# The leaky rectifier of a feed-forward layer as one activation with a slope

## The chip, the core and the metric

The kernel runs on one core of a Trainium2 chip. The metric is the device time of one execution in microseconds. TensorE (PE) multiplies matrices, VectorE (DVE), ScalarE (ACT) and GpSimd (POOL) work on tiles of 128 partitions, and SyncE (SP) issues the transfers.

## The reference

Attention keeps the 32 largest scores of each row, then two feed-forward layers follow. The first has a leaky rectifier with slope 0.01, the second a squared rectifier.

```python
# q, k, v: (4, 8, 576, 64); 2304 tokens of 512 features; both layers 512 -> 2048 -> 512
scores = scale * np.matmul(q, k.transpose(0, 1, 3, 2))
kth = np.partition(scores, -top_k, axis=-1)[..., -top_k:-top_k + 1]     # top_k = 32
scores = np.where(scores >= kth, scores, -1000000000.0)
attn = softmax(scores); x = attn @ v                                    # as (2304, 512)
h = x @ w_in;  g = np.maximum(0.01 * h, h);       x = g @ w_out         # first layer
h = x @ w_in2; r = np.maximum(h, 0.0); g = s * (r * r) + b
out = g @ w_out2                                                        # second layer
```

## The kernel before

**Precision.** TensorE multiplies float16. Each operand is held as the sum of two float16 halves: the high half is the rounded value, the low half the rest. A product takes three matmuls (high by high, high by low, low by high). Weights arrive as float64 bits and are turned into halves in the first 200 us; those of the first layer stay on the chip, those of the second go to device memory and are streamed back for each block, except two pairs that stay ("kept").

**Attention.** A unit is a pair of heads for 128 queries; there are 18 tiles of 128 queries and 4 units in each, 72 in all. For a unit and head, TensorE computes 128 x 576 scores (line 768) and ScalarE copies them to s (L774). VectorE finds the 32 largest by four rounds of MAX8 (L786) with three MATCH_REPLACE8 between (L795). ScalarE takes the exponential (L808), and VectorE's mask (L811) keeps what is at least the 32nd largest score and sums it. ScalarE and GpSimd make the halves (L865, L869), a transposing DMA turns them (L873; the first 7 units go through TensorE instead), TensorE multiplies by the values (L897), and VectorE scales the result into x (L904), after a small GpSimd step (L820, L823) and a reciprocal (L826).

**The feed-forward layers.** The 18 tiles form 14 blocks: ten of one tile and four of two (blocks 10 to 13). A layer of a block begins with `rows_in`: ScalarE's square with a sum (L940), a power of two on VectorE (L298, L303), a scaled copy (L944), the high half (L947), GpSimd's low half (L950), and a transposing DMA (L968), for each tile. Then it goes through groups g of 512 columns of h: TensorE computes h (L1022, in packets of 12 matmuls), the rectifier makes it g in halves, and TensorE adds g times the second weights to acc (L1093, packets of 3 matmuls). The second layer's rows come from acc of the first.

**The rectifier of the first layer**, for each of its 72 groups: ScalarE's a1 (L1050) reads h with a positive scale and clips, a2 (L1054) does it with -0.01 times the scale, into a tile of ring r2 that lies in the common tile `early`. GpSimd's a3 subtracts one from the other (L1058). Then a4 (L1067) makes the high half on ScalarE and a5 (L1070) the low half on GpSimd:

```python
nc.scalar.activation(box["r1"], box["h"], AF.Relu, scale=cg[:, 2 * l, 3, gi:gi + 1])
nc.scalar.activation(box["r2"], box["h"], AF.Relu, scale=cg[:, 1, 3, g * nf // 4:g * nf // 4 + 1])
nc.gpsimd.tensor_tensor(box["r1"], box["r1"], box["r2"], op=ALU.subtract)
```

In the second layer a1 clips, GpSimd squares for the low half (L1062), and ScalarE squares for the high one (L1067).

**What sets the order.** A planner, `Plan`, holds each step with its engine, a price in us, what it waits for, the buffers of rings that it takes, and a key. `order()` plays all steps through in time: whenever an engine is free, it takes the ready step with the lowest key. The instructions of each engine are then written in that order, and at run time each engine works through its own list in order. The feed-forward steps of a1 to a5 have the lowest keys of all (-200); matmuls of the layers have keys that grow with the block and the layer, so a change of prices or steps in one place can change the order anywhere behind it. The tables of offsets at the top of the file (`KO`, `W0`, `WD`) are keys, too.

Of the kernel before, what the change touches and what calls it, by code (L numbers as in the profile page):

```python
# [21 lines left out]
# buffers of each ring of tiles  # L22
# [3 lines left out]
# who takes the low halves of the weights: P the tensor engine, D the vector engine, G GpSimd  # L26
WM = {"1i": "PPP", "1o": "P", "2i": "PG", "2o": "DP"}
ORDER = ("1i", "1o", "2i", "2o")
# loads of weights before all others
WF = 0  # L30
EB = 7
# rows of which layers are turned by a transfer
# [3 lines left out]
# offsets of keys: loads of weights, halves of weights, keys, values, queries, the first units  # L36
KO = {"wl": 8.18, "wh": 1.24, "k": -17.94, "v": -14.26, "q": -62.89, "u0": -7.18, "u1": -1.77, "u2": -1.7, "kt": -23.91, "qh": -4.87}
NB = 10
# pairs of blocks of the second layer that stay on the chip
NRES = 2  # L40
DEBUG = []
# from the end of a step to the start of one that waits for it
# [5 lines left out]
# from the issue of a transfer to its start  # L48
# [8 lines left out]
class Plan:  # L57
    """Steps of single engines with what they need, put into a static order: each engine takes, whenever it is free,
    the ready step with the lowest key. A token is a buffer of a ring, taken by its first step and free after its last."""
# [7 lines left out]
    def token(self, ring):  # L67
        self.by_tok.append([ring, 0])
        return len(self.by_tok) - 1
# [19 lines left out]
    def order(self):  # L89
# [17 lines left out]
        while events:  # L107
# [13 lines left out]
            for e, q in ready.items():  # L121
                while q and free[e] <= now + 1e-9:
# [16 lines left out]
                    if e == "SP":  # L139
                        # transfers are issued one by one, wait for each other and take their time  # L140
                        end = moved = max(now + self.issue[n] + LAG, moved) + self.dur[n]
# [25 lines left out]
def kernel(  # L167
# [35 lines left out]
    def open_phase(name):  # L203
        # the pool of the weights' way in makes room for the one of the weights' way round
# [9 lines left out]
    # rings in a common tile: what the beginning needs lies where something else comes later  # L214
# [42 lines left out]
    # ------------------------------------------------ constants  # L257
# [26 lines left out]
    def inv2(dst, src):  # L284
        # dst = 1 / src for powers of two
        nc.vector.tensor_scalar(dst.bitcast(I32), src.bitcast(I32), -1.0, float(254 << 23), op0=ALU.mult, op1=ALU.add)

    def chain(eng, todo, deps, key, take=(), use=()):
        # steps one after the other: (price, function)
# [5 lines left out]
    def pow2_steps(dst, src, step=1, dur=0.07):  # L295
        # dst = a power of 2 (of 4: step 2) with dst * sqrt(src) in [2^-1/2, 2^1/2) ([2^-3/2, 2^1/2))
# [10 lines left out]
    # ------------------------------------------------ the weights: float64 bits to float32, then to scaled halves  # L307
    # a scale for each four blocks
# [15 lines left out]
    for m, f in order:  # L324
# [14 lines left out]
        def w_shift(m=m, f=f):  # L339
            # the low seven exponent bits and the fraction move up by three  # L340
# [4 lines left out]
        def w_rest(m=m, f=f):  # L345
            # the fraction's next bits, rounded, as an integer in the last place
# [862 lines left out]
```

## Time and profile before

| | us |
|---|---|
| median of 3 runs | 1252.0 |
| lowest run | 1249.91 |
| highest run | 1602.58 |
| span of the profiled execution, first to last instruction | 1250.3 |
| busy in it: TensorE, VectorE, ScalarE, GpSimd | 1070.3, 1036.9, 827.4, 842.1 |

No time of the profiled execution other than its span is given; the span lies between two of the runs. The third run, 1602.58, stands far from the other two and is not used. Busy times overlap, since the engines run side by side; a step counts for the end only where other engines wait for it.

### The profile page before, as it was taken

The numbers are of one execution on the slowest core, as the hardware profiler recorded it, in microseconds if no ns is written. First come the engines' busy times: TensorE is split into PE (matmuls) and PEld (weight loads), VectorE is DVE, ScalarE is ACT, GpSimd is POOL, SyncE is SP. The second block draws the span as 40 slices with busy tenths as digits, with TensorE's granted clock in tenths as the row PEclk, the third lists the DMA queues.
The fourth block names the chain that finished last, engine by engine and source line by source line (L and its number), as shares of the span: only waits on it lengthen the run. The fifth ranks groups of instructions, "written<-read, shape, count | busy, mean of one in ns | idle before, by whom it ended". The sixth has DMA issues, their size and how long they took to land.

```text
span 1250.3 us, 27997 instructions
## 1 busy us (share of the span) xinstructions
PE 1070.3 (86%) x10520; PEld 735.6 (59%) x10520; DVE 1036.9 (83%) x2437; ACT 827.4 (66%) x1427; POOL 842.1 (67%) x1126
## 2 busy tenths in 40 slices
PE   2666767788888988988998989789989799899998
PEld 1333334556666766665776666566566466666665
DVE  4999899999989999999999999889999999800000
ACT  7887998866577766667876665558876565444321
POOL 5776555657678877677887776658887666655542
PEclk9877898999999999999999999989999999999999
DMA  7767776478889898888899797988445568510444
GB/s 180 237 217 213 198 199 198 148 165 211 218 158 240 199 263 183 220 201 223 221 237 248 165 249 162 261 231 195 83 80 114 149 162 228 153 26 18 133 162 161
DMA packets 362408, 228.39 MB, mean 183 GB/s; under 512 B 276512, under 2 KB 301088, under 8 KB 362272
## 3 DMA queue, kind: packets, MB, share of 16 engines
q1 hardware_dynamic: 362272, 226.61, 71.5%
q8 instruction: 82, 1.34, 0.5%
q14 instruction: 54, 0.44, 0.1%
HBM read 151.52 MB, written 13.11 MB: 132 GB/s over the span
## 4 chain that ended last, share of the span: by engine, by line
DVE 24%; PE 22%; DMA 17%; POOL 9%; issue 4%; ACT 4%; SPq 1%; DVEq 0%; POOLq 0%; ACTq 0%
DMA ahl<-ehl 10%; DVE mx L786 9%; PE acc L1093 9%; PE h L1022 9%; DVE wk L795 8%; DVE em L811 5%; POOL ehl L869 3%; DMA st_o<-sc_2o 2%; PE pv L897 2%; POOL g L1070 2%; DMA qn<-in_q_dram 1%; POOL r L1058 1%; PE sc L768 1%; DMA vn<-in_v_dram 1%; DMA st_i<-sc_2i 1%
## 5 line engine op out<-in xcount | busy, mean ns | idle before, releaser
L786 DVE MAX8 mx<-wk 128x8 f32<-128x576 f32 x432 | 311.3, 744 | 0.0
L1093 PEld LDWEIGHTS <-g 128*128 128x128 f16 x1728 | 159.5, 98 | 141.0 <-issue 23.7
L1022 PE MATMUL h<-early,wreg 128*128 128x128 f16 (+1 forms) x2688 | 224.2, 235 | 5.1 <-DMA early<-xhl 3.5
L1022 PEld LDWEIGHTS <-wreg 128*128 128x128 f16 x2688 | 194.3, 98 | 52.8 <-issue 5.1
L1093 PE MATMUL acc<-wreg,g 128*128 128x512 f16 x864 | 222.8, 380 | 0.2 <-DVE o L1152 0.2
L795 DVE MATCH_REPLACE8 wk<-mx,wk 128x576 f32<-128x576 f32 x288 | 212.7, 741 | 0.0
L1093 PE MATMUL acc<-st_o,g 128*128 128x512 f16 x756 | 194.5, 379 | 12.9 <-DMA st_o<-sc_2o 12.6
L869 POOL TENSOR_TENSOR ehl<-em,ehl 128x576 f16<-128x576 f32 x130 | 168.0, 1298 | 50.1 <-ACT ehl L865 49.7
L1022 PE MATMUL h<-xT,st_i 128*128 128x128 f16 (+1 forms) x2352 | 198.5, 236 | 2.3 <-DMA st_i<-sc_2i 2.0
L1022 PEld LDWEIGHTS <-st_i 128*128 128x128 f16 x2352 | 170.3, 99 | 45.5 <-DMA st_i<-sc_2i 5.0
L1050 ACT ACTIVATE r<-h,cg 128x512 f32<-128x512 f32 x144 | 98.3, 683 | 93.7 <-PE h L1022 74.8
L811 DVE SCALAR_TENSOR_TENSOR em<-s,mx,em 128x576 f32<-128x576 f32 x144 | 155.0, 1087 | 0.3 <-ACT em L808 0.2
L865 ACT CAST ehl<-em 128x576 f16<-128x576 f32 x130 | 86.4, 668 | 93.0 <-DVE em L811 67.1
L808 ACT ACTIVATE em<-s,st,est 128x576 f32<-128x576 f32 x144 | 121.8, 861 | 18.9 <-POOL st L789 14.9
L1067 ACT ACTIVATE g<-r 128x512 f16<-128x512 f32 x144 | 89.9, 626 | 64.1 <-PE acc L1093 44.5
L897 PE MATMUL pv<-vhl,ahl 128*128 128x64 f16 (+3 forms) x2160 | 86.6, 201 | 49.8 <-DMA ahl<-ehl 47.6
L897 PEld LDWEIGHTS <-ahl 128*128 128x128 f16 (+1 forms) x2160 | 79.6, 104 | 71.9 <-DMA ahl<-ehl 66.8
L1058 POOL TENSOR_TENSOR r<-r,early 128x512 f32<-128x512 f32 x72 | 93.6, 1300 | 38.2 <-ACT early L1054 37.9
L1062 POOL TENSOR_TENSOR early<-r 128x512 f32<-128x512 f32 x72 | 75.7, 1052 | 62.1 <-ACT r L1050 61.4
L774 ACT COPY s<-sc 128x576 f32<-128x576 f32 x144 | 91.5, 636 | 35.0 <-PE sc L768 31.8
L768 PE MATMUL sc<-kT,qT 128*128 128x288 f16 (+1 forms) x640 | 99.2, 297 | 11.2 <-ACT s L774 9.7
L786 DVE MAX8 mx<-s 128x8 f32<-128x576 f32 x144 | 107.0, 746 | 0.3 <-ACT s L774 0.3
(191 smaller groups left out, 1741.0 us busy)
## 6 DMA issues: line engine op xcount, KB each, us to landing
st_i<-sc_2i SPq DMA_DIRECT2D x98, 512.0 KB, 4.8
st_o<-sc_2o SPq DMA_DIRECT2D x98, 512.0 KB, 4.8
raw_2i<-in_moe_w_in_dram SPq DMA_DIRECT2D x16, 512.0 KB, 4.9
wreg<-in_moe_w_in_dram SPq DMA_DIRECT2D x16, 512.0 KB, 5.7
raw_1o<-in_moe_w_out_dram SPq DMA_DIRECT2D x16, 512.0 KB, 4.0
raw_2o<-in_moe_w_out_dram SPq DMA_DIRECT2D x16, 512.0 KB, 4.1
qn<-in_q_dram SPq DMA_DIRECT2D x16, 256.0 KB, 4.8
sc_2i<-hl_2i SPq DMA_DIRECT2D x16, 256.0 KB, 2.4
```

The costliest lines, as they stand in the source:

```text
L768: nc.tensor.matmul(pt[a, c, 0:288], lhsT=qT[u][:, h, z, a], rhs=kT[b, p][:, 576 * h + 288 * c:576 * h + 288 * c + 288], start=(z == 0), st ...
L774: nc.scalar.copy(sc[u, h], box["pt"][:, :, 0:288])
L786: nc.vector.max(out=mx[u][:, h, r, :], in_=wk[u, h] if r else flat(sc[u, h]))
L795: nc.vector.match_replace(out=wk[u, h], in_to_replace=mx[u][:, h, r, :], in_values=src, imm_value=NEG)
L808: nc.scalar.activation(em[u][:, h, :], flat(sc[u, h]), AF.Exp, bias=st[u][:, h:h + 1], scale=est[:, 0, u:u + 1])
L811: nc.vector.scalar_tensor_tensor(em[u][:, h, :], flat(sc[u, h]), mx[u][:, h, 3, 7:8], em[u][:, h, :], op0=ALU.is_ge, op1=ALU.mult, accum_o ...
L869: nc.gpsimd.tensor_tensor(ehl[u][:, 1, a], em[u][:, h, :], ehl[u][:, 0, a], op=ALU.subtract)
L897: nc.tensor.matmul(pt[a, o0:o1], lhsT=ahl[u][:, za, blk * P + a.start:blk * P + a.stop], rhs=vt[:, zv, v0:v1], start=(i == 0 and za == 0 a ...
L1022: nc.tensor.matmul(box["h"][:, n * T:(n + 1) * T], lhsT=w[:, ew, c, :], rhs=src[:, ex, c, :], start=(c == 0 and ew == 0 and ex == 0), stop ...
L1050: nc.scalar.activation(box["r1"], box["h"], AF.Relu, scale=cg[:, 2 * l, 3, gi:gi + 1])
L1058: nc.gpsimd.tensor_tensor(box["r1"], box["r1"], box["r2"], op=ALU.subtract)
L1093: nc.tensor.matmul(accs[i, l, tt], lhsT=ghl[i, l, g][:, eg, n * T + tt * P:n * T + (tt + 1) * P], rhs=w[:, ew], start=(f == 0 and eg == 0 ...
```

## The change

The first layer's a1 becomes an activation Prelu with alpha 0.01 from h into r1, with the same positive scale. Its a2 and the subtraction in a3 are gone, and with them the first layer's use of ring r2 and the one VectorE instruction that prepared the negative scale. The second layer's steps stay. The planner's tables and the prices of the other steps are the same, and the order is planned anew. (Comments that go are left out of the diff.)

```diff
@@ finals1
         nc.vector.scalar_tensor_tensor(cg[:, 0, 3, :], cg[:, 0, 2, :], 2.0 ** -12, cg[:, 1, 2, :], op0=ALU.mult, op1=ALU.mult)
-        nc.vector.tensor_scalar(cg[:, 1, 3, :], cg[:, 0, 3, :], -0.01, None, op0=ALU.mult)
@@ layer
             def a1(g=g, box=box):
                 box["r1"] = ring("r1", [P, 512], F32, f"r1_{i}_{l}_{g}")
                 gi = g * nf // 4
-                nc.scalar.activation(box["r1"], box["h"], AF.Relu, scale=cg[:, 2 * l, 3, gi:gi + 1])
-
-            def a2(g=g, box=box):
-                box["r2"] = ring("r2", [P, 512], F32, f"r2_{i}_{l}_{g}")
-                nc.scalar.activation(box["r2"], box["h"], AF.Relu, scale=cg[:, 1, 3, g * nf // 4:g * nf // 4 + 1])
-
-            def a3(g=g, box=box):
                 if l == 0:
-                    nc.gpsimd.tensor_tensor(box["r1"], box["r1"], box["r2"], op=ALU.subtract)
+                    nc.scalar.activation(box["r1"], box["h"], AF.Prelu, scale=cg[:, 0, 3, gi:gi + 1], alpha=0.01)
                     box["v"] = box["r1"]
                 else:
-                    box["r2"] = ring("r2", [P, 512], F32, f"r2_{i}_{l}_{g}")
-                    nc.gpsimd.tensor_tensor(box["r2"], box["r1"], box["r1"], op=ALU.mult)
-                    box["v"] = box["r2"]
+                    nc.scalar.activation(box["r1"], box["h"], AF.Relu, scale=cg[:, 2, 3, gi:gi + 1])
+
+            def a3(g=g, box=box):
+                box["v"] = ring("r2", [P, 512], F32, f"r2_{i}_{l}_{g}")
+                nc.gpsimd.tensor_tensor(box["v"], box["r1"], box["r1"], op=ALU.mult)
...
-            t1, t2, tg = token("r1"), token("r2"), token("g")
+            t1, tg = token("r1"), token("g")
+            t2 = token("r2") if l else None
             ka = -200.0 + 0.001 * g
             if l == 0:
                 x = add(ACT, 0.571, a1, [x, fin1], ka, take=[t1], use=[th])
-                x = add(ACT, 0.571, a2, [x], ka, take=[t2], use=[th])
-                x = y = add(POOL, 1.225, a3, [x], ka, use=[t1, t2])
                 x = add(ACT, 0.52, a4, [x], ka, take=[tg], use=[t1])
                 x = add(POOL, 1.113, a5, [x], ka, use=[t1, tg])
```

In the changed file the lines behind this place are seven lower (L1093 is L1086), and those of attention one lower.

Three places of the new order. The first is VectorE at unit 38, before: em_9651 is the mask tile of unit 38 (its two masks stand further up), pv_9937 its product, em_9845 the mask tile of the next unit.

```order
L811 SCALAR_TENSOR_TENSOR em_9845,st_9660<-s_0_9492,mx_9659,em_9845 128x576
L712 TENSOR_SCALAR cqt<-cqt 128x1
L786 MAX mx_9659<-wk_1_9742 128x8
L786 MAX mx_9897<-s_0_9720 128x8
L811 SCALAR_TENSOR_TENSOR em_9845,st_9660<-s_1_9588,mx_9659,em_9845 128x576
L795 MATCH_REPLACE wk_0_9923<-mx_9897,s_0_9720 128x576
L786 MAX mx_9897<-s_1_9784 128x8
L826 RECIPROCAL st_9660<-st_9660 128x2
L786 MAX mx_9897<-wk_0_9923 128x8
L904 TENSOR_TENSOR x_9_9571<-pv_9937,st_9407 128x128
```

The same place of the changed kernel: pv_9774 is unit 38's product, em_9691 the mask tile of the next unit.

```order
L785 MAX mx_9595<-wk_1_9668 128x8
L298 TENSOR_SCALAR pw<-xss_7_9736 128x1
L785 MAX mx_9595<-wk_0_9619 128x8
L303 TENSOR_SCALAR pw<-pw 128x1
L794 MATCH_REPLACE wk_1_9668<-mx_9595,wk_1_9668 128x576
L903 TENSOR_TENSOR x_9_9422<-pv_9774,st_9399 128x128
L785 MAX mx_9595<-wk_1_9668 128x8
L810 SCALAR_TENSOR_TENSOR em_9691,st_9596<-s_0_9425,mx_9595,em_9691 128x576
```

The step that takes the product stood behind both masks of the next unit and stands ahead of them now.

The second place is ScalarE near the end, where the last block (13, tiles 16 and 17) goes from its first layer's acc to the rows of its second layer. Before (r_12_1_3 is block 12, second layer, group 3):

```order
L1067 ACTIVATE g_1_1_16927<-r_12_1_1_16876 128x512
L1050 ACTIVATE r_12_1_3_16951<-h_1_3_16914,cg 128x512
L940 ACTIVATE xhl_16_16983,xss_16_16982<-acc_0_0_16642 128x512
L944 ACTIVATE xs_16_16990<-acc_0_0_16642,pw 128x512
L947 CAST xhl_16_16983<-xs_16_16990 128x512
L940 ACTIVATE xhl_17_17007,xss_17_17006<-acc_0_1_16647 128x512
L944 ACTIVATE xs_17_17016<-acc_0_1_16647,pw 128x512
L947 CAST xhl_17_17007<-xs_17_17016 128x512
L1067 ACTIVATE g_1_2_17051<-r_12_1_2_16912 128x512
L1067 ACTIVATE g_1_3_17058<-r_12_1_3_16951 128x512
L1050 ACTIVATE r_12_1_4_17061<-h_1_4_16953,cg 128x512
```

In the changed kernel:

```order
L1061 ACTIVATE g_0_6_17020<-r_13_0_6_16980 128x512
L1061 ACTIVATE g_0_7_17035<-r_13_0_7_17015 128x512
L939 ACTIVATE xhl_16_17072,xss_16_17071<-acc_0_0_16887 128x512
L939 ACTIVATE xhl_17_17075,xss_17_17074<-acc_0_1_16906 128x512
L943 ACTIVATE xs_16_17079<-acc_0_0_16887,pw 128x512
L943 ACTIVATE xs_17_17083<-acc_0_1_16906,pw 128x512
L946 CAST xhl_16_17072<-xs_16_17079 128x512
L946 CAST xhl_17_17075<-xs_17_17083 128x512
L1053 ACTIVATE r_13_1_0_17140<-h_1_0_17099,cg 128x512
L1061 ACTIVATE g_1_0_17142<-r_13_1_0_17140 128x512
L1053 ACTIVATE r_13_1_1_17173<-h_1_1_17127,cg 128x512
```

Before, steps of block 12's second layer stand on both sides of the turn; now only block 13's own steps do.

The third place is TensorE at the same turn, of each packet one row. Before, behind the last acc of block 13's first layer (16647) come packets of block 12's second layer (its rows are xT_12), 6 of h and 19 of acc, until the first one of block 13's second layer (xT_13):

```order
L1093 MATMUL acc_0_1_16647<-wreg,g_0_7_16853 128x512
...
L1022 MATMUL h_1_5_16992<-xT_12_16671,st_i_16949 128x256
...
L1093 MATMUL acc_1_0_17010<-kept_o_2908,g_1_0_16824 128x512
...
L1022 MATMUL h_1_6_17114<-xT_12_16671,st_i_17091 128x256
...
L1022 MATMUL h_1_7_17151<-xT_12_16671,st_i_17109 128x256
...
L1022 MATMUL h_1_0_17188<-xT_13_17030,kept_i_2851 128x256
```

In the changed kernel (16887 and 16906 are the two acc of block 13's first layer, kept_i is a weight pair that stays on the chip):

```order
L1086 MATMUL acc_0_0_16887<-wreg,g_0_7_17035 128x512
...
L1086 MATMUL acc_0_1_16906<-wreg,g_0_7_17035 128x512
L1021 LDWEIGHTS kept_i_3005
L1021 MATMUL h_1_0_17099<-xT_13_17089,kept_i_3005 128x256
...
L1021 LDWEIGHTS st_i_16726
L1021 MATMUL h_1_1_17127<-xT_13_17089,st_i_16726 128x256
```

The packets of block 12 that lay between have moved ahead of block 13's first layer, and the second layer of block 13 follows its first layer at once.

## Rows read from the trace of the kernel before

**Rows 1.** Busy time by stretches, all engines, with counts, granted clock and DMA.

```profile
core 0: us, PE busy (x) PEld busy (x) DVE busy (x) ACT busy (x) POOL busy (x), PEclk, DMA share, GB/s
31.00:215.00 184.00, 129.14 (x717) 69.07 (x716) 176.06 (x392) 161.47 (x251) 116.47 (x132) 0.86 0.73 211
215.00:1094.00 879.00, 783.65 (x8752) 563.33 (x8750) 839.30 (x1972) 591.83 (x1046) 638.53 (x891) 0.99 0.79 192
1094.00:1250.00 156.00, 151.34 (x1033) 98.92 (x1031) 8.58 (x31) 51.84 (x87) 70.46 (x62) 1.00 0.33 100
```

**Rows 2.** The page's costliest groups: busy us, mean ns, idle before; VectorE.

```profile
L786 DVE MAX8 mx<-wk 128x8 f32<-128x576 f32 x432 | 311.3, 744 | 0.0
...
L811 DVE SCALAR_TENSOR_TENSOR em<-s,mx,em 128x576 f32<-128x576 f32 x144 | 155.0, 1087 | 0.3 <-ACT em L808 0.2
```

**Rows 3.** VectorE's waits, 31 to 1094 us: total us, times, longest.

```profile
DVE x L904 <- PE pv L897: 19.2, 19, 2.8
DVE st L826 <- POOL st L823: 6.1, 10, 1.5
```

**Rows 4.** VectorE in order of time, near the end: start, us, instruction.

```profile
1098.27 0.29 DVE L904 TENSOR_TENSOR x<-pv,st 128x128 f32<-128x128 f32 x1 [8.18 <-PE pv L897]
...
1245.96 1.41 DVE L1152 SCALAR_TENSOR_TENSOR o<-acc,fin,bc 128x512 f32<-128x512 f32 x2 [31.63 <-PE acc L1093]
```

**Rows 5.** TensorE in order of time, in the tail.

```profile
1169.70 0.81 PE L1093 MATMUL acc<-wreg,g 128*128 128x512 f16 x3
1170.35 1.47 PE L1022 MATMUL h<-xT,st_i 128*128 128x256 f16 x12
1171.66 0.81 PE L1093 MATMUL acc<-wreg,g 128*128 128x512 f16 x3
```

**Rows 6.** The page's costliest groups: the rectifier's steps.

```profile
L1050 ACT ACTIVATE r<-h,cg 128x512 f32<-128x512 f32 x144 | 98.3, 683 | 93.7 <-PE h L1022 74.8 <-POOL g L1070 17.2 <-POOL st L820 0.6
...
L1054 ACT ACTIVATE early<-h,cg 128x512 f32<-128x512 f32 x72 | 49.2, 683 | 1.1 <-POOL g L1070 1.1
...
L1058 POOL TENSOR_TENSOR r<-r,early 128x512 f32<-128x512 f32 x72 | 93.6, 1300 | 38.2 <-ACT early L1054 37.9 <-POOL vhl L666 0.2
```

**Rows 7.** Instructions of line 811: duration in ns, least, median, greatest.

```profile
L811 DVE SCALAR_TENSOR_TENSOR em<-s,mx,em x144: 775/873/1901, 35.1 to 1086.7; 128x576 f32<-128x576 f32 x144
```

**Rows 8.** VectorE in order of time, 645 to 650 us.

```profile
645.74 0.80 DVE L811 SCALAR_TENSOR_TENSOR em<-s,mx,em 128x576 f32<-128x576 f32 x1
...
647.81 1.64 DVE L811 SCALAR_TENSOR_TENSOR em<-s,mx,em 128x576 f32<-128x576 f32 x1
```

**Rows 9.** GpSimd in order of time, from before 644 to 650 us.

```profile
644.52 0.19 POOL L789 TENSOR_TENSOR st<-mx,est 128x1 f32<-128x1 f32 x1 [0.69 <-DVE mx L786]
646.45 1.16 POOL L950 TENSOR_TENSOR xhl<-xs,xhl 128x512 f16<-128x512 f32 x1 [1.73 <-ACT xhl L947]
647.56 1.27 POOL L1058 TENSOR_TENSOR r<-r,early 128x512 f32<-128x512 f32 x1
```

**Rows 10.** Busy time by stretches, line 1058 alone.

```profile
215.00:1094.00 879.00, 78.69 (x61) 0.99 0.79 192
```

**Rows 11.** ScalarE in order of time, block 12's turn to its second layer.

```profile
1132.13 0.60 ACT L940 ACTIVATE xhl<-acc 128x512 f16<-128x512 f32 x1
...
1136.69 0.64 ACT L947 CAST xhl<-xs 128x512 f16<-128x512 f32 x1
```

**Rows 12.** GpSimd in order of time, the same turn.

```profile
1138.65 1.16 POOL L950 TENSOR_TENSOR xhl<-xs,xhl 128x512 f16<-128x512 f32 x1
```

**Rows 13.** Tile xT from 1094 us on: the transposing transfers from issue to landing.

```profile
DMA to landing us min/median/max: 3.0/3.1/3.1
```

**Rows 14.** TensorE in order of time, 799 to 817 us.

```profile
811.36 1.78 PE L897 MATMUL pv<-vhl,ahl 128*128 128x128 f16 x27 [2.98 <-DMA ahl<-ehl]
```

**Rows 15.** Busy time by stretches around that wait; PEclk is third from the end.

```profile
810.50:817.30 6.80, 5.94 (x49) 4.05 (x51) 5.54 (x14) 1.34 (x2) 2.33 (x5) 0.50 1.00 316
```

**Rows 16.** Instructions of line 707: the one load of an activation table.

```profile
L707 ACT ACT_TABLE_LOAD  x1: 1283/1283/1283, 0.7 to 0.7; - x1
```

## Prediction

> **What bounds the kernel now.** I read the busy time by stretches first, because one share for the whole span mixes stages with different limits. From 31 to 215 and from 215 to 1094 us VectorE is busy 176.1 of 184 and 839.3 of 879 us, so the attention stage belongs to it; after 1094 us it does 8.6 of 156 us and TensorE 151.3 [rows 1]. So there are two stages with two owners: VectorE's top-32 search until about 1094, then a tail of feed-forward matmuls. Next, VectorE's groups: the search itself (MAX8 on the working copy alone 311.3 us) and the mask of line 811, 144 times at a mean of 1087 ns [rows 2]. Third, what VectorE waits for in attention: mostly the result of attention times values, at line 904, 19.2 us in 19 waits; then a reciprocal that needs GpSimd, 6.1 us [rows 3]. It is never held there by the two steps that the change removes. Last, the tail: the last attention result is taken at 1098.27, the last output at 1245.96 [rows 4]; between them a packet of 12 matmuls into h starts the next one 1.31 us later and one of 3 into acc 0.65 us later [rows 5]. In the order of before, 51 packets of the first kind and 123 of the second stand behind the last attention product: 51 x 1.31 + 123 x 0.65 = 146.8 us, which is nearly all of these 147.7 us. The tail is TensorE's packed work and has no waits in it.
>
> **Removed work.** Per group of the first layer one ScalarE activation and one GpSimd subtraction go: 72 of each, 49.2 us and 93.6 us [rows 6]. The activation that stays becomes the one with a slope. Its cost is not in the trace; the nearest rows are the same shape with the plain rectifier, 683 ns [rows 6], and I take that. Were it twice as long, 49 us would come back on ScalarE, which is busy 591.8 of 879 us in attention [rows 1] and would hide it. So on these two engines the change gives room and not time: neither owns a stage. One tiny multiplication of four columns on VectorE goes too, below 0.2 us.
>
> **The mask on VectorE.** What the room is worth in attention goes through the mask. It takes 775 ns at best and up to 1901 [rows 7]. At 645.74 it takes 0.80 us while GpSimd is idle but for the last 0.1; at 647.81 it takes 1.64 us, beside the removed subtraction that began at 647.56 [rows 8, 9]. So a GpSimd operation on two float inputs stretches it. The whole stretch is 144 x (1.087 - 0.775) = 45 us; that is the most that could come back, and zero the least if other GpSimd work moves into the gap. The subtraction makes 78.7 us of GpSimd's 638.5 us between 215 and 1094 [rows 1, 10], 12%; 12% of 45 us is 5 us, which I take.
>
> **The attention result on VectorE.** The order is planned anew, and VectorE comes to line 904 sooner after the mask. For unit 38 the order shows it: before, both masks of the next unit stand ahead of that step, afterwards none. Counting MAX8, MATCH_REPLACE8 and mask instructions between a unit's second mask and line 904, over the 64 units that go by the transposing DMA, the mean falls from 15.4 to 14.2, and units with 13 or fewer rise from 19 to 31. What lies under that time (casts, GpSimd halves, the DMA, the product) gets a little shorter too, as the engines are freer, but not the DMA. Bounds: all 19.2 us vanish, or they double. 19.2 us over 64 units is 0.3 us each; 12 more tight units cost 3.6 us, so I take +3. If VectorE stands there, the next unit's search is queued behind it.
>
> **The tail.** Here the order differs more than the diff suggests. Before, the first layer of block 13 (the last one) and the second layer of block 12 overlap: while rows of block 13 go from acc through ScalarE, GpSimd and DMA to become the second layer's input, TensorE has block 12's second layer to do: 6 packets of h and 19 of acc stand between block 13's two layers, 6 x 1.31 + 19 x 0.65 = 20 us by [rows 5]. After the change block 12's second layer comes first, and behind the last acc of block 13's first layer TensorE has only block 13's second layer, which needs that very input. The cover is gone. Its price from the steps of this chain: before, for block 12, the first square starts at 1132.13 and the second cast ends at 1137.33, with 1.7 us of other activations between [rows 11]; without them 3.5 us. The first half on GpSimd starts 0.1 us behind the first cast, at 3.1 us; the two, 1.16 us each [rows 12], end at 5.4. The transposing DMA lands 3.1 us after its issue [rows 13]: 8.5 us from the first square, which itself starts 0.2 us after a matmul that ends 0.65 us ahead of the last. So TensorE idles 8 us; with the other work between as before it would be 1132.13 to 1139.81 + 3.1, or 10.8 us. SyncE has both transposes ahead of any load that waits for this layer, so nothing delays them.
> The idle engine also loses clock: after a wait of 2.98 us [rows 14], the granted clock is 0.50, so 1.2 GHz, for 6.8 us [rows 15]. Half of 6.8 us is 3.4 us; none and twice that are the ends, and I take one such stretch. Finally, one more h packet and one more acc packet stand behind the last attention product: 1.31 + 0.65 = 2 us.
>
> **The sum.** The profiled execution's span is 1250.3 us, no other time of it is given, and the median of the runs is 1252.0, so they agree within 0.2%. 1250.3 - 5 (mask) + 3 (line 904) + 2 (more work in the tail) + 8 (uncovered chain) + 3.4 (clock) = 1261.7, so 1262 us: the change takes out 143 us of work and the kernel gets about 1% slower.
>
> **Rivals.**
> *Freed engines pay more.* Every wait at line 904 shrinks with the shorter queues, and the subtraction accounts for twice its share of the stretched masks, as it is one of the few GpSimd steps that read two float operands and write float. Then -10 for masks and -15 at line 904: 1250.3 - 25 + 13.4 = 1239 us. For it: ScalarE and GpSimd queues stand between mask and product. Against it: the long part there is the DMA, and the planner has already spent the slack. Chance 0.19.
> *VectorE stands at line 904.* The tighter slots cost another 0.3 us on each of 64 units, so the 19.2 us double: 1250.3 - 5 + 19 + 13.4 = 1278 us. It decides the verdict from about 18 us of added waiting. For it: the count above, and 31 tight units; against it: in the trace before also units with long slots wait, so the slot is not the only cause. Chance 0.2.
> *The slope needs another table.* If the function with a slope were not in the table that the exponential uses, ScalarE would load tables to and fro: a load takes 1283 ns [rows 16], twice per group is 72 x 2 x 1.283 = 185 us, of which two thirds, ScalarE's busy share in attention, would show: 1262 + 123 = 1385 us. The order of the changed kernel has one load, at its start, as before; chance 0.02.
> The Trainium skill, "ScalarE: Activation LUTs", section "Table sets: the hidden batching unit", says that functions come in named sets and a switch between sets costs a load, and does not say which set holds the function with a slope; by that rule the change could end at 1385 us. The trace agrees on the load's price, 1283 ns, and shows only one.
> *The cover isn't needed.* TensorE finishes block 13's first layer earlier because its chain is shorter, but the tail has no other work to put in; the 8 us only vanish if the tail before has a hidden wait as long. The packet count (146.8 of 147.7 us) leaves no room. It would give 1251 us; chance 0.04.
>
> **How the numbers follow.** The forecast, 1262, gets 0.55. Its own spread is 1250 to 1272, from the mask's 0 to 10 us, the clock's 0 to 6.8 and the 8 to 10.8 us of the chain. About 2% (25 us) is what a measurement of this kernel can tell from no change: 1227 and 1277 are the limits. Slower than 1277: nearly half of the second rival, the table rival, and a tail of the forecast in which the whole planned order fits worse, together 0.17. Below 1227 only a much larger mask gain leads: 0.03. The range from 1241 to 1282 leaves one in ten out at each end.
>
> **What would show it.** Right: the mask's mean falls from 1087 to about 1050 ns; line 904 waits about 22 us; one TensorE gap of about 8 us between the last acc of the first layer and the first h of the second, followed by the 16 h and 32 acc packets of that layer, 16 x 1.31 + 32 x 0.65 = 42 us, with granted clock 0.5 beside it; about 149 us of packets behind the last attention product. Wrong: no such gap, line 904 waiting under 10 or over 35 us, a second table load, or an activation with a slope well over 690 ns that something waits for.

## The result and the profile after

| | us |
|---|---|
| changed kernel, median of 4 runs (1263.5 to 1269.5) | 1266.6 |
| kernel before, beside it, median of 3 runs (1249.9 to 1255.9; a fourth, 1602.6, stands far off and is left out) | 1252.0 |
| ratio, 95% interval | 1.0118 [1.0079, 1.0157] |
| predicted: 1262 in a range of 1241 to 1282 | |
| profiled execution of after: own time, span | 1269.45, 1267.6 |

The change takes two of the rectifier's five steps out of 72 groups, and the kernel is 1.2% slower. The removed work is gone where it was: the stretches of after, read as [rows 1].

```profile
core 0: us, PE busy (x) PEld busy (x) DVE busy (x) ACT busy (x) POOL busy (x), PEclk, DMA share, GB/s
215.00:1094.00 879.00, 783.66 (x8750) 564.61 (x8748) 838.52 (x1975) 560.22 (x987) 554.73 (x826) 0.98 0.77 185
1094.00:1250.00 156.00, 144.47 (x978) 94.74 (x977) 8.23 (x29) 42.81 (x72) 57.17 (x52) 0.97 0.42 127
```

GpSimd is busy 84 us less in attention and ScalarE 32 us less; VectorE, which owns that stage, is busy as before. In the tail TensorE is busy 144.5 us of 156 where it was 151.3. VectorE's group of the mask on the page (busy us, mean ns, idle before), then its waits and its last steps in order of time, as [rows 2 to 4]:

```profile
L810 DVE SCALAR_TENSOR_TENSOR em<-s,mx,em 128x576 f32<-128x576 f32 x144 | 151.9, 1065 | 2.5 <-ACT em L807 2.5
```

```profile
DVE x L903 <- PE pv L896: 20.5, 17, 4.4
...
DVE st L825 <- POOL st L822: 2.7, 5, 1.4
```

```profile
1100.54 0.29 DVE L903 TENSOR_TENSOR x<-pv,st 128x128 f32<-128x128 f32 x1 [4.19 <-PE pv L896]
...
1263.27 1.41 DVE L1145 SCALAR_TENSOR_TENSOR o<-acc,fin,bc 128x512 f32<-128x512 f32 x2 [49.91 <-PE acc L1086]
```

The last attention product is taken 2.3 us later than before, and the tail, from there to the start of VectorE's last output step, is 162.7 us instead of 147.7. TensorE's waits in the tail (1094 us to the end: total us, times, longest), and TensorE in order of time at the turn of block 13:

```profile
PE h L1021 <- DMA xT<-xhl: 8.3, 1, 8.3
PE h L1021 <- DMA st_i<-sc_2i: 1.5, 2, 1.1
PE acc L1086 <- DMA st_o<-sc_2o: 0.8, 2, 0.7
```

```profile
1199.68 11.17 PE L1086 MATMUL acc<-wreg,g 128*128 128x512 f16 x51
1219.13 5.28 PE L1021 MATMUL h<-xT,kept_i 128*128 128x256 f16 x24 [8.28 <-DMA xT<-xhl]
1224.20 4.49 PE L1021 MATMUL h<-xT,st_i 128*128 128x256 f16 x36
1228.53 0.81 PE L1086 MATMUL acc<-kept_o,g 128*128 128x512 f16 x3
```

There is one long gap, of 8.28 us, between the last acc of the first layer and the first h of the second. What fills it stands on three other engines: ScalarE, GpSimd, and the issue on SyncE.

```profile
1210.24 0.60 ACT L939 ACTIVATE xhl<-acc 128x512 f16<-128x512 f32 x1 [6.43 <-PE acc L1086]
...
1212.62 1.14 ACT L946 CAST xhl<-xs 128x512 f16<-128x512 f32 x2
```

```profile
1213.32 2.26 POOL L949 TENSOR_TENSOR xhl<-xs,xhl 128x512 f16<-128x512 f32 x2 [8.21 <-ACT xhl L946]
```

```profile
1214.50 2.65 SPq L967 DMA_TRANSPOSE xT<-xhl  x2
```

From the first square at 1210.24 to the first matmul at 1219.13 it is 8.9 us, where the prediction worked out 8.5. The clock beside the gap, by stretches:

```profile
1209.50:1219.00 9.50, 1.35 (x7) 0.39 (x4) 1.82 (x12) 3.51 (x8) 2.26 (x2) 0.78 0.29 55
1219.00:1226.00 7.00, 6.87 (x37) 4.98 (x38) 0.00 (x0) 1.32 (x2) 0.73 (x1) 0.57 0.00 0
```

Right behind the gap the granted clock is 0.57 on average, mostly the lower level of 1.2 GHz. The activation with a slope costs what the plain one does, 687 ns at the median (least, median, greatest below), and there is one load of a table, as in [rows 16]:

```profile
L1050 ACT ACTIVATE r<-h,cg x72: 664/687/697, 216.6 to 1199.9; 128x512 f32<-128x512 f32 x72
```

```profile
L706 ACT ACT_TABLE_LOAD  x1: 1283/1283/1283, 0.7 to 0.7; - x1
```

### The profile page after: what moved, and what is told of

Its sections match the earlier page's. It is cut to its first block, busy times and chain, and to the rows that moved or that the text cites. A ratio compares the mean times of both kernels' runs of the same rounds, so it can differ in the third digit from the quotient of the medians.

```text
span 1267.6 us, 27844 instructions
## 1 busy us (share of the span) xinstructions
PE 1073.5 (85%) x10520; PEld 737.0 (58%) x10520; DVE 1037.4 (82%) x2436; ACT 787.6 (62%) x1355; POOL 748.7 (59%) x1054
## 4 chain that ended last, share of the span: by engine, by line
DVE 41%; PE 23%; DMA 16%; POOL 7%; ACT 6%; issue 5%; SPq 1%; POOLq 0%; ACTq 0%; DVEq 0%
DVE mx L785 14%; DVE wk L794 12%; PE h L1021 9%; PE acc L1086 8%; DMA ahl<-ehl 8%; DVE em L810 6%; PE pv L896 2%; DMA st_o<-sc_2o 2%; POOL ehl L868 2%; DMA st_i<-sc_2i 2%; POOL g L1064 2%; PE sc L767 1%; DMA qn<-in_q_dram 1%; DVE raw_2i L353 1%; DMA kT<-khl 1%
## 5 line engine op out<-in xcount | busy, mean ns | idle before, releaser
L1086 PEld LDWEIGHTS <-g 128*128 128x128 f16 x1728 | 160.2, 99 | 138.9 <-issue 25.2
L868 POOL TENSOR_TENSOR ehl<-em,ehl 128x576 f16<-128x576 f32 x130 | 167.4, 1292 | 100.5 <-ACT ehl L864 100.0
L1086 PE MATMUL acc<-wreg,g 128*128 128x512 f16 x864 | 224.6, 381 | 1.1 <-DVE o L1145 0.8
L1086 PE MATMUL acc<-st_o,g 128*128 128x512 f16 x756 | 197.1, 382 | 10.3 <-DMA st_o<-sc_2o 10.3
L810 DVE SCALAR_TENSOR_TENSOR em<-s,mx,em 128x576 f32<-128x576 f32 x144 | 151.9, 1065 | 2.5 <-ACT em L807 2.5
L1064 POOL TENSOR_TENSOR g<-r,g 128x512 f16<-128x512 f32 x72 | 86.2, 1197 | 100.8 <-ACT g L1061 99.5
L1145 DVE SCALAR_TENSOR_TENSOR o<-acc,fin,bc 128x512 f32<-128x512 f32 x18 | 13.2, 744 | 128.8 <-PE acc L1086 128.8
L794 DVE MATCH_REPLACE8 wk<-mx,s 128x576 f32<-128x576 f32 x144 | 106.9, 742 | 0.0
```

Of the source, the lines that this page charges most:

```text
L794: nc.vector.match_replace(out=wk[u, h], in_to_replace=mx[u][:, h, r, :], in_values=src, imm_value=NEG)
L810: nc.vector.scalar_tensor_tensor(em[u][:, h, :], flat(sc[u, h]), mx[u][:, h, 3, 7:8], em[u][:, h, :], op0=ALU.is_ge, op1=ALU.mult, accum_o ...
L868: nc.gpsimd.tensor_tensor(ehl[u][:, 1, a], em[u][:, h, :], ehl[u][:, 0, a], op=ALU.subtract)
L1064: nc.gpsimd.tensor_tensor(ghl[i, l, g][:, 1], box["v"], ghl[i, l, g][:, 0], op=ALU.subtract)
L1086: nc.tensor.matmul(accs[i, l, tt], lhsT=ghl[i, l, g][:, eg, n * T + tt * P:n * T + (tt + 1) * P], rhs=w[:, ew], start=(f == 0 and eg == 0 ...
```

## The experiments

The question was how the 14.6 us (1266.6 - 1252.0) split between the instruction itself, the planned order in attention, and the order at the end. Every diff below is against the changed kernel, but for the two of the loads one by one, which are against the first variant. In all of them the first layer has the activation with a slope.

**The old order with the new instruction.** The planner still counts the two steps that are gone, with their old prices and the buffer of ring r2, but they issue nothing. The order of the engines is then that of before, minus the removed instructions.

```diff
-            t2 = token("r2") if l else None
+            t2 = token("r2")
...
+                x = add(ACT, 0.571, lambda: None, [x], ka, take=[t2], use=[th])
+                x = y = add(POOL, 1.225, lambda: None, [x], ka, use=[t1, t2])
```

> The changed instructions in the order of the kernel before: the planner still counts the two steps that are gone, but they issue nothing. Theory (the time was lost through the new order of the tail): the cover is back, so no TensorE gap over 1 us between the layers of the last block, 147 to 148 us from the last attention product to the last output, masks shorter by 3 to 5 us, total 1245 to 1251, below both kernels. Rival A (the activation with a slope or the emptier queues lose the time by themselves): 1260 or more with any order. Rival B (the freed engines are worth nothing): 1250 to 1254, masks at 1087 ns.

Measured: 1245.5 us (12 runs), ratio to before 0.996 [0.9935, 0.9984]. The page's group of the mask, and the last steps of VectorE:

```profile
L810 DVE SCALAR_TENSOR_TENSOR em<-s,mx,em 128x576 f32<-128x576 f32 x144 | 146.6, 1029 | 0.5 <-ACT em L807 0.2
```

```profile
1092.87 0.29 DVE L903 TENSOR_TENSOR x<-pv,st 128x128 f32<-128x128 f32 x1 [8.83 <-PE pv L896]
...
1241.88 1.41 DVE L1147 SCALAR_TENSOR_TENSOR o<-acc,fin,bc 128x512 f32<-128x512 f32 x2 [32.95 <-PE acc L1088]
```

The masks take 8.4 us less than in [rows 2] (146.6 against 155.0), the last product is taken 5.4 us earlier, and the tail is about as long as before (149.0 us). So the instruction, with the two steps gone, gains a little by itself, and the loss is the order's.

**The cover given back.** In the new order, the key of block 13's first layer is lowered by 3.5. TensorE's order differs only behind the last product: 84 h and 57 acc matmuls of block 12 lie again between the two layers of block 13.

```diff
+        if l == 0 and i == len(blocks) - 1:
+            base -= 3.5
```

> The changed kernel with one key changed: the first layer of the last block gets a key below the second layer of the block before it, which changes the order only behind the last attention product. Theory: the 8.3 us gap and the 2.4 us of low clock go, the rest stays: 1266.6 - 10.7 = 1256, tail of 150 to 152 us. Rival A (the tail is longer because more packets stand in it, or because the streamed weights come late): 1262 or more. Rival B (the loss sits in attention): 1264 or more.

Measured: 1258.2 us (12 runs), 1.0047 [1.0028, 1.0067]. The wait for xT is not among TensorE's waits in the tail any more, which begin with

```profile
PE acc L1088 <- DMA st_o<-sc_2o: 1.5, 2, 1.2
PE h L1023 <- DMA st_i<-sc_2i: 1.1, 1, 1.1
```

and the tail is 152.0 us. So 8.5 us of the loss hang on the uncovered turn (9.5 where both ran side by side, below). Of the rest, 12.6 us to the variant with the old order, the tail holds only 3; the other 9.6 lie ahead of the last product.

**The gap filled.** 36 matmuls of 128x512 that nobody reads stand in front of the last layer's first h, so that TensorE keeps busy while it waits for xT.

```diff
+                    if f == 0 and l == 1 and i == len(blocks) - 1:
+                        keep = ring("tp", [P, 512], F32, "keep")
+                        for _ in range(36):
+                            nc.tensor.matmul(keep, lhsT=ones16, rhs=whl("1o", 0)[:, 0], start=True, stop=True)
```

> The changed kernel with 36 matmuls of 512 columns, whose result nobody reads, on TensorE ahead of the second layer of the last block, 36 x 0.213 = 7.7 us, inside the gap of 8.3 us. Theory (part of the loss is the clock after the gap): granted clock 1.0 behind the gap, the first 24 matmuls of the layer in 2.6 us instead of 5.1, total 2.4 us less, 1264. Rival (the matmuls are slow there for another reason, such as the freshly landed rows): 24 matmuls still take over 4 us, total 1266 to 1268.

Measured: 1265.0 us, 1.0108 [1.0059, 1.0157]. TensorE in order of time, and the stretch behind the gap:

```profile
1209.96 7.93 PE L1018 MATMUL keep<-wreg,ones 128*128 128x512 f16 x36
1218.45 2.78 PE L1025 MATMUL h<-xT,kept_i 128*128 128x256 f16 x24 [0.56 <-DMA xT<-xhl]
1221.07 4.09 PE L1025 MATMUL h<-xT,st_i 128*128 128x256 f16 x36
1225.00 0.81 PE L1090 MATMUL acc<-kept_o,g 128*128 128x512 f16 x3
```

```profile
1218.00:1226.00 8.00, 7.55 (x67) 6.50 (x68) 0.00 (x0) 2.64 (x4) 3.40 (x4) 1.00 0.13 31
```

At the full clock the 24 matmuls into h take 2.62 us to the next start instead of 5.07, and the 36 behind them 3.93 instead of 4.33: the lower clock costs 2.9 us in rows. The medians differ by 1.6 us, which is not clear of their scatter (1262.2 to 1269.9 here, 1263.5 to 1269.5 without the filling), so the time alone decides nothing; the rows are the theory's. TensorE now waits 3.5 us for the streamed weights (2.3 and 1.2) where it waited 2.3, so part of the 2.9 us is lost again.

**A GpSimd step added behind the rectifier.** 72 subtractions in place of a tile whose last reader is done; nobody reads the result.

```diff
+                if l == 0:
+                    nc.gpsimd.tensor_tensor(box["r1"], box["r1"], box["r1"], op=ALU.subtract)
```

> The changed kernel with GpSimd's load put back: behind each low half of the first layer a subtraction in place on r1, whose result nobody reads, 72 in all. Same order else. Theory (GpSimd's load stretches the mask): its mean goes from 1065 ns back to 1085 or more, 3 us on VectorE, total 1268 to 1272. Rival (the mask's 3 us came from the order, not from the load): mean below 1070, total 1265 to 1268.

Measured: 1285.8 us, 1.0278 [1.0238, 1.0318], far more than expected. ScalarE's waits in attention show why (total us, times, longest):

```profile
ACT r L1050 <- POOL r L1066: 21.8, 16, 2.4
```

The step holds the tile that a later activation writes into; in the changed kernel that activation waits 7.1 us for the tile (10 times, at most 1.3). The mask's mean rises to 1103 ns, as the theory had it, and VectorE is busy 1024.3 us up to the last product instead of 1015.7, but it is also idle for 60.5 us instead of 53.9. So the run mixes GpSimd's load with a longer wait and gives no price for either.

**The loads one by one, in the old order.** The first kernel with one of the two empty steps filled again, each into ring r2, which nobody reads: the GpSimd subtraction, or the ScalarE activation.

```diff
-                x = y = add(POOL, 1.225, lambda: None, [x], ka, use=[t1, t2])
+                x = y = add(POOL, 1.225, lambda box=box, k=f"r2_{i}_{l}_{g}": nc.gpsimd.tensor_tensor(box["d"] if "d" in box else ring("r2", [P, 512], F32, k), box["r1"], box["r1"], op=ALU.subtract), [x], ka, use=[t1, t2])
```

> The kernel of e1_old_order (changed instructions, order of before) with GpSimd's removed load put back in the old place: 72 subtractions of r1 from itself into ring r2, which nobody reads and nothing waits for. Theory (the 6 us of e1_old_order come from GpSimd's load on VectorE's mask): mask mean from 1029 back to 1080 ns or more, total 1250 to 1253. Rival (they come from the shorter chain or from ScalarE): mask below 1050 ns, total 1244 to 1248.

```diff
-                x = add(ACT, 0.571, lambda: None, [x], ka, take=[t2], use=[th])
+                x = add(ACT, 0.571, lambda box=box, gi=g * nf // 4, k=f"r2_{i}_{l}_{g}": nc.scalar.activation(box.setdefault("d", ring("r2", [P, 512], F32, k)), box["h"], AF.Relu, scale=cg[:, 0, 3, gi:gi + 1]), [x], ka, take=[t2], use=[th])
```

> The kernel of e1_old_order with ScalarE's removed load put back in the old place: 72 activations of h into ring r2, which nobody reads. Theory: ScalarE is no bound, mask stays at 1020 to 1040 ns, total within 2 us of e1_old_order, 1244 to 1248. Rival (ScalarE's queue decides when the halves for the attention product are ready): waits of line 904 rise by 5 us or more, total 1250 or more.

Measured: with the subtraction 1251.8 us, 0.9993 [0.9973, 1.0012]; with the activation 1247.3 us, 0.9948 [0.9928, 0.9968]. GpSimd's load brings the time of before back, ScalarE's does not. But the mask's mean hardly rose with the subtraction (page's group, and the added line):

```profile
L810 DVE SCALAR_TENSOR_TENSOR em<-s,mx,em 128x576 f32<-128x576 f32 x144 | 147.1, 1033 | 0.3 <-ACT em L807 0.2
```

```profile
L1072 POOL TENSOR_TENSOR early<-r x72: 1031/1041/1617, 218.8 to 1157.6; 128x512 f32<-128x512 f32 x72
```

The added step, which reads one tile twice, takes 1041 ns at the median; the removed one, which read two tiles, took 1277 in the kernel before:

```profile
L1058 POOL TENSOR_TENSOR r<-r,early x72: 1266/1277/1797, 218.2 to 1158.2; 128x512 f32<-128x512 f32 x72
```

So it is a shorter step than the one removed. The time is the theory's and the mask's mean the rival's, so neither holds as it stood; what the step did to VectorE is counted under "What the shared load is".

**Other prices for the new activation.** The planner counts 0.571 us for it. Two kernels change only this number, to 0.60 and to 0.69, which is nearly what the trace shows.

```diff
-                x = add(ACT, 0.571, a1, [x, fin1], ka, take=[t1], use=[th])
+                x = add(ACT, 0.6, a1, [x, fin1], ka, take=[t1], use=[th])
```

> The changed kernel, with the planner's price of the new activation 0.60 instead of 0.571. The instructions are the same, the order differs from early on, and block 12's second layer lies again between the two layers of block 13. Theory (the order and not the instruction loses the time): no TensorE gap over 1 us in the tail, total 1243 to 1260, depending on how the attention part falls out. Rival (any newly planned order with the shorter chain loses about 13 us): 1262 or more.

> The changed kernel, with the planner's price of the new activation 0.69, which is what the trace shows for it (687 ns). Again another order, again with cover in the tail. Theory: no gap over 1 us in the tail, total 1243 to 1260, and not the same as with 0.60, since attention's slots fall otherwise. Rival: 1262 or more with either price.

Measured: 1264.9 us, 1.0104 [1.0085, 1.0124], with 0.60, and 1248.2 us, 0.9964 [0.9949, 0.9978], with 0.69. So the first time is the rival's and the second the theory's: not every new order loses 13 us, and a covered turn alone doesn't save them. Both turns are covered. With 0.60 the last product is early but more is left behind it: 708 h and 408 acc matmuls, 59 x 1.31 + 136 x 0.65 = 165.7 us by [rows 5], against 146.8 before. VectorE's last steps give 167.3:

```profile
1088.22 0.29 DVE L903 TENSOR_TENSOR x<-pv,st 128x128 f32<-128x128 f32 x1 [6.92 <-PE pv L896]
...
1255.49 1.41 DVE L1145 SCALAR_TENSOR_TENSOR o<-acc,fin,bc 128x512 f32<-128x512 f32 x2 [31.90 <-PE acc L1086]
```

**Half old, half new.** The empty steps are counted in all blocks but the last, or only in blocks 0 to 7 (condition `i < 8`).

```diff
-            t2 = token("r2") if l else None
+            t2 = token("r2") if l or i < len(blocks) - 1 else None
...
+                if i < len(blocks) - 1:
+                    x = add(ACT, 0.571, lambda: None, [x], ka, take=[t2], use=[th])
+                    x = y = add(POOL, 1.225, lambda: None, [x], ka, use=[t1, t2])
```

> The first-layer rectifier is the new activation in all blocks; the planner counts the two empty steps in every block but the last (13). TensorE's order is that of the old kernel up to its last packets, 612 h and 369 acc matmuls stand behind the last product as before, and 84 h and 57 acc matmuls of block 12 lie between the two layers of block 13. Theory (what counts is the attention part of the order and a covered turn): like the variant with the old order, 1245 us, last product taken near 1093, no TensorE wait for xT. Rival (the planner's view of block 13 itself is what costs): 1255 us or more with the turn or the weight stream waiting.

> The planner counts the two empty steps only in blocks 0 to 7, so TensorE's order is the old one up to its row 12773 (about 60% of the program) and a third one behind it; the turn of block 13 is covered (60 h and 57 acc matmuls between), and 636 h and 375 acc matmuls stand behind the last product, 150.7 us by packets against 146.8. Theory (time = when the last product is taken + packets behind it + gaps): last product near 1093, tail 153, so about 1249 us. Rival (any order planned without the empty steps is worse throughout): 1258 us, as with the moved key.

Measured: 1249.3 us, 0.9971 [0.9948, 0.9994], and 1252.7 us, 1.0006 [0.999, 1.0022]. The first is 4 us above the theory's 1245 and well below the rival's 1255; its turn is covered, and its tail is 150.1 us. The second lies between its two forecasts: its tail is 154.8 us, and 1093 + 154.8 with the 6.2 us of the table below would be 1254. The "about 1249" was added up without those 6 us. An order planned without the empty steps from block 8 on isn't worse throughout, which is what the rival had said.

**Two kernels profiled once more.** The changed kernel and the one with the moved key, unchanged, on one chip.

> The changed kernel with the key of block 13's first layer 3.5 lower, once more, for a second profile: the first profile's execution (1254.5 us) was the fastest of its twelve, 3.7 us below their median. Theory (the attention part of the new order is about 5 us later than that of the old one): last product taken at 1098 to 1100 and a tail of 152 us. Rival (the remainder lies in the tail): last product at 1096, tail of 156 us.

> The changed kernel once more, on the same chip, for a second profile: last product taken at 1098 to 1100 and a tail of 162 us with one wait of 8.3 us for xT by the theory; by the rival (the remainder lies in the tail) last product at 1096 and a longer tail.

Measured: 1258.2 us, 1.0034 [1.0015, 1.0052], and 1267.7 us, 1.0117 [1.0091, 1.0144]. The tails repeat within 1.3 us (152.2 and 161.4), the last product is taken at 1100.41 and 1099.37: as the theory had it, the rest lies in attention.

**Nearly all of them in one table** (without the run that mixed two causes). Own time less the start of the last output row is 6.2 us (1269.45 - 1263.27). So the median less a profile's tail and 6.2 is the usual time of the last product. The masks' time (with their accumulator reads) and VectorE's busy time are those of the windows from 31 us to the last product, of which three kernels' rows follow; the masks above 1.2 us are counted in VectorE's order of time.

| kernel | median | tail | last product | masks | VectorE busy | masks > 1.2 us |
|---|---|---|---|---|---|---|
| before | 1252.4 | 147.7 | 1098.5 | 156.0 | 1015.4 | 48 |
| after, two profiles | 1266.6, 1267.7 | 162.7, 161.4 | 1097.7, 1100.1 | 152.9, 151.7 | 1015.7, 1011.7 | 48, 49 |
| moved key, two profiles | 1258.2, 1258.2 | 152.0, 152.2 | 1099.9, 1099.8 | 150.4, 152.4 | 1010.3, 1014.8 | 46, 48 |
| gap filled | 1265.0 | 161.2 | 1097.6 | 152.2 | 1013.7 | 50 |
| old order | 1245.5 | 149.0 | 1090.3 | 147.6 | 1006.1 | 37 |
| old order + activation | 1247.3 | 148.2 | 1092.9 | 142.6 | 1002.6 | 31 |
| old order + subtraction | 1251.8 | 148.9 | 1096.7 | 148.1 | 1010.3 | 38 |
| all blocks but the last | 1249.3 | 150.1 | 1093.0 | 144.0 | 1003.8 | 34 |
| blocks 0 to 7 | 1252.7 | 154.8 | 1091.7 | 146.2 | 1007.1 | 36 |
| price 0.60 | 1264.9 | 167.3 | 1091.4 | 144.0 | 1004.8 | 38 |
| price 0.69 | 1248.2 | 149.7 | 1092.3 | 150.0 | 1009.0 | 41 |

(1252.4 is about the median of before beside these runs, 1251.9 to 1252.5.) Of after and of the old order, first all of VectorE and then line 810 alone:

```profile
31.00:1100.54 1069.54, 1015.67 (x2367) 0.96 0.76 189
31.00:1100.54 1069.54, 152.89 (x288) 0.96 0.76 189
```

```profile
31.00:1092.87 1061.87, 1006.10 (x2362) 0.96 0.78 196
31.00:1092.87 1061.87, 147.56 (x288) 0.96 0.78 196
```

And of before:

```profile
31.00:1098.27 1067.27, 1015.36 (x2363) 0.96 0.78 195
31.00:1098.27 1067.27, 156.01 (x288) 0.96 0.78 195
```

The six kernels in another order and without a subtraction take the last product at 1090 to 1093 us. Of the orders without it, only that of after, in five profiles, is as late as before, and it alone has as many stretched masks. By the profiles, after takes the last product 7.7 and 6.5 us later than the old order; the masks are 5.3 and 4.2 us of that, VectorE's other work 4.2 and 1.4, and its idle time -1.9 and +0.9. Summed up from the rows in order of time, GpSimd works on the low halves of attention (L868) and of the layers' rows (L949) beside masks for 19.6 and 9.8 us in after, 14.2 and 4.7 us in the old order; with the low halves of g (L1064) it is 50.1 us against 37.5. The removed subtraction had 14.1 us beside masks in the trace before, and the same three kinds 38.7. In the new order other GpSimd work moved into most of its place.

## Why the prediction was right, and where its sizes were off

**The direction and the tail: right.** Forecast were 8 us of uncovered chain, 3.4 of clock and 2 of more work, 13.4 together. Measured in the tail are 15.0 and 13.7 us (two profiles). The first are 8.3 of gap, 2.9 of clock in rows, 2.0 of packets, and 1.5 of longer waits for streamed weights (1.5 + 0.8 us), a term that the prediction did not have. Before, TensorE's waits in the tail begin with 0.8 us for the same stream:

```profile
PE h L1022 <- DMA st_i<-sc_2i: 0.8, 1, 0.8
PE acc L1093 <- DVE o L1152: 0.3, 1, 0.3
```

The key moved back brought 8.5 and 9.5 us, where the gap and the clock are 11.2 in rows. The clock's term, 2.9 in rows against 3.4, was not clear of the scatter in medians. The 42 us forecast for block 13's second layer are 44.1, from 1219.13 to 1263.27, or 41 at full clock.

**The mask: right cause, wrong by two errors that cancel in part.** The step "12% of 45 us is 5 us" is twice too small for the removal itself: in the trace before, the masks that start inside the subtraction are 9.2 us longer by it (counted below), with the old order the masks fall by 8.4 us, and over the six kernels of the table in another order to a mean of 145.7, by 10. In after they fall by 3.1 and 4.3 only, because the lower end that the prediction named for this term, other GpSimd work moving into the place, is what the new order does for the most part. The forecast mean of 1050 ns stood at 1065 and 1057. The subtraction also held other steps of VectorE, about 5.5 us before, for which the prediction has no term; that too is not kept: VectorE's time outside the masks is 862.8 and 859.9 us in after and 858.5 in the old order, against 859.4 before.

**Line 904: the forecast rise is hardly there.** The step of "31 tight units" forecast +3 us. Up to the last product the waits there are 20.5 us in the first profile and 19.2 in the second, against 19.2 [rows 3], and the last one is 4.0 us shorter (4.19 against 8.18 [rows 4]). So the count of tight units does not give this wait. VectorE's whole idle time up to the last product still rose: 1069.5 - 1015.7 = 53.9 us against 1067.3 - 1015.4 = 51.9, and 56.7 in the second profile. So the sum of attention, forecast at -2, came out at -1 to +2 (last product at 1097.7 and 1100.1 against 1098.5).

**The base: 2 us low.** The sum started from the span, 1250.3 us. Own time is longer than the span by 1.85 us in after, and the median of before is 1251.9 to 1252.5. With 1252.2 the same terms give 1263.6, and the difference forecast, +11.4, stands against +14.6 and +15.3.

**The rivals.** "The slope needs another table" fell with one load in the trace; "the cover isn't needed" with the 8.3 us gap. "VectorE stands at line 904" fell with +1.3 and 0 us there, where it needed 19. "Freed engines pay more" fell for this order, but what it said of the masks was right of the instruction: about twice the subtraction's share is what the old order gives back, and in that order, with the tail covered, the kernel is faster by 0.4%. What removes the gain is where the planner puts the remaining steps.

**What the shared load is.** [Rows 8, 9] show a mask at 1.64 us beside a GpSimd subtraction and at 0.80 without. The Trainium skill, "GPSIMD Engine Reference", section "Specifications", says that GpSimd shares its SBUF interfaces with VectorE and contends with VectorE instructions that have two SBUF inputs. The traces agree: MAX8, with one such input, takes 0.72 to 0.76 us throughout before, and the masks, with two, 0.78 to 1.90 [rows 7]; those above 1.2 us number 48 before and 31 to 41 in the six kernels without the subtraction in another order.

The rows in order of time show what the contention is: the mask waits for the end of the GpSimd step. In [rows 8, 9] the subtraction ends at 648.83 (647.56 + 1.27) and the mask 0.62 us later. In the kernel with the subtraction put back, VectorE and then GpSimd:

```profile
588.04 1.60 DVE L810 SCALAR_TENSOR_TENSOR em<-s,mx,em 128x576 f32<-128x576 f32 x1
```

```profile
587.99 1.03 POOL L1072 TENSOR_TENSOR early<-r 128x512 f32<-128x512 f32 x1
```

Again the mask ends 0.62 us behind the step. It holds whatever is left of the step: in all 14 profiles, 784 masks start inside a GpSimd step longer than 1 us of which 0.19 us or more is left, and 769 of them end 0.61 to 0.63 us behind it. (14 of the others, one in each profile, start at about 76 us inside one early step.) With GpSimd idle a mask takes 0.79 to 0.82 us. Small steps wait in the same way. Before, a VectorE product of one column, which takes 0.14 us at best, takes 1.09 and ends with the subtraction:

```profile
569.79 1.09 DVE L1138 TENSOR_TENSOR fin<-pw 128x1 f32<-128x1 f32 x1
```

```profile
569.59 1.28 POOL L1058 TENSOR_TENSOR r<-r,early 128x512 f32<-128x512 f32 x1 [0.27 <-ACT early L1054]
```

So the price of a GpSimd step lies in the masks and other such steps that start inside it, and it can be counted. Against 0.805 us for each mask, the masks before are 40.7 us longer: 9.2 through the 16 that start inside the subtraction, and 31.5 through GpSimd's other steps. Without the subtraction the other steps cost 32.3 us in the old order, but 37.5 and 36.3 in the order of after. That is why the old order keeps the masks' gain and the new one loses about half of it or more. The subtraction put back holds 8 masks, for 3.7 us, and other VectorE steps for about 3.6, together 7.3. GpSimd's other steps cost the masks 29.1 us there, 3.2 less than in the old order without it, so the masks' mean hardly rose and VectorE is busy 4.2 us longer. The last product came 4.8 us later by the profiles and 6.4 by the medians. Why the other steps cost less there, one profile doesn't tell.

## What to carry to other kernels

Where a planner sets a static order, an edit that removes steps is two edits: the work and the order. Time them apart by letting the planner count empty steps; here the work was worth about -6 us and the order about +21. Read an order by three numbers: when the owner of the first stage is done, how many packets are left behind that, and whether something covers each turn from one layer to the next. Where VectorE owns a stage, count its steps with two SBUF inputs that start inside a GpSimd step, and not GpSimd's busy share. A planner's prices move the result: 0.571, 0.60 and 0.69 us for one 687 ns step gave 1267, 1265 and 1248 us. With one order for each price, it is not shown that the true price gives the better order. The version to keep is the new activation with the old order, at 1245.5 us, or with the price as measured, at 1248.2.

## What was not expected of the hardware

A VectorE step of one column can wait for most of a GpSimd step: 1.09 us, where it takes 0.14 at best. A GpSimd subtraction of 128x512 with one tile as both operands takes 1041 ns at the median, with two tiles 1277. One kernel's executions scatter by 5 us and more (the moved key: 1254.5 to 1263.0), and by the profiles the scatter lies in attention: two of it take the last product at 1096.3 and 1100.4 us, with tails of 152.0 and 152.2. One profile's end of attention is therefore no measure of a few us; its tail is.
